# New engine lists and gate forms for a gated linear recurrence followed by a soft mixture of experts

## The chip, the cores and the metric

The kernel runs on one core of one Trainium2 chip. A core has five engines that run at the same time, each working through its own list of instructions strictly in order: TensorE (PE; its weight loads are shown apart as PEld), VectorE (DVE), ScalarE (ACT), GpSimd (POOL) and SyncE (SP), which here only issues transfers. Engines wait for each other and for transfers through semaphores. An instruction that waits holds up everything behind it in its engine's list.

The metric is the device time of one execution in microseconds (us). Less is better.

## The reference

Four sequences of 5056 tokens with 256 channels pass through a gated linear recurrence. Its output, taken as 20224 tokens, passes through a soft mixture of 8 experts with 4 slots each (32 slots).

```python
sig_r = 1.0 / (1.0 + np.exp(-r_gate))
sig_i = 1.0 / (1.0 + np.exp(-i_gate))
a_t = np.exp(8.0 * sig_r * np.log(a_base))
x_gated = np.sqrt(np.maximum(1.0 - a_t * a_t, 1e-06)) * sig_i * x
for t in range(S):
    h = a_t[:, t] * h + x_gated[:, t]
    y[:, t] = h

logits = y @ phi                               # tokens x 32 slots
d = softmax of logits over the tokens
slot_input = d.T @ y                           # 32 x 256
slot_out[e] = relu(slot_input[e] @ w1[e]) @ w2[e]   # 1024 hidden, per expert
c = softmax of logits over the slots
out = c @ slot_out
```

Everything is 32-bit floating point. The three inputs x, r_gate and i_gate have 20.7 MB each, the expert weights 16.8 MB, the output 20.7 MB.

## The kernel before

**Tiling.** The tokens are cut into 40 quads of 512 tokens (the last one is shorter). Quads are joined into 21 units: quad 0 alone, then two quads each, then the last one alone. A name such as SC7.1 means: scan, unit 7, half 1 of the 256 channels. Names with U, SR, SI, TR, TY, YC and D carry the number of a quad, names with LG, LE, LD, TE, ES, AC, AE and DM the number of one of 12 groups (nine of two units, three of one), over which the token softmax runs on.

**What is done for a quad or unit, in order.**

- Dr, Di, Dx (SP, line 708): the loads of r gate, i gate and x, 512 KB each. r and i go to seven `st` tiles, x to one of twenty double-size `b` tiles.
- TR (PE, line 781) turns the r gate so that channels lie on partitions; SR (ACT, line 792) takes its tanh; EX (ACT, line 860) makes the decay a of it.
- SI (ACT, line 807 or 805) makes the input gate from the i gate. U (line 828 or 830) multiplies it with x. TU (PE, line 902) turns the product.
- SQ (POOL or DVE, line 847) squares a; RT (ACT, line 883) takes the square root of 1 - a². ST (DVE, line 920) multiplies it with the turned product; SC (DVE, line 937) runs the recurrence as a scan along the tokens and needs the scan of the unit before it.
- TY (PE, line 960) turns the result back, YC copies it out of PSUM (ACT, line 974, or DVE, line 976).
- LG (PE, line 1022) computes the logits of a group; LE and LD, TE, ES, AC and AE carry a running maximum, exponentials and the weighted sum of tokens into the 32 slots. CT (line 1472), CM, CS, CE, RR (line 1503), RB, RC, CN, CH and CL compute the softmax over the slots and split it into two parts of lower precision.

**Behind the last scan** a serial part merges the running sums (MT to SL), runs the first expert layer (L1), relu (HS, HT, HR) and the second (L2), and makes the output table (SO to BD). The weights w10 to w27 (first digit: layer, second: expert) are loaded into `b` or `st` tiles as these come free. Then HP, HE, OT, OE (lines 1561 to 1607) compute the output and OD (line 1627) stores it.

**Four forms of the input gate.** `IV` has one letter for each quad. With D, ACT takes a tanh, and one DVE instruction with two inputs in SBUF computes (tanh + 1) times x (line 828). With P, POOL adds one first (line 818), and a plain product on POOL follows (line 830). With E, POOL multiplies tanh and x into the i gate's tile, and PE adds x while it turns the product: TU then has twice as many transposes. With S, ACT takes the sigmoid itself, from another set of its functions, and a plain product follows. The root's scale and the floor in ST go with the form.

**What sets the order.** `ORDER` (lines 91 to 160) has one written list of task names for each engine. A planner (`Planner.run`) plays these lists with a cost for each task. Its times decide which tile is given to which task, in what order the code is emitted, and where PE gets filler transposes (line 1226) while it would stand idle; the order on each engine is that of its list. Emission derives all waits from the tiles that are read and written.

```python
o = raw("i" if how == "E" else "x", q)[:, : n * D]
if how == "D":
    nc.vector.scalar_tensor_tensor(o, a, 1.0, b, op0=ALU.add, op1=ALU.mult)
else:
    eng.tensor_tensor(out=o, in0=a, in1=b, op=ALU.mult)
...
nms = ("i", "x") if gate_of(q) == "E" else ("x",)
```

## Time and profile before

| what | us |
|---|---|
| median of 3 runs | 302.67 (301.88 to 302.75) |
| the profiled execution | 304.15 |
| its span, first to last instruction | 302.4 |
| busy PE / DVE / ACT / POOL in it | 262.7 / 244.9 / 247.8 / 195.3 |

The profile is of one execution. Its span runs from the first to the last instruction, so the execution's own time is longer. Times of instructions are counted from the start of the span. Register, branch, semaphore and transfer-issuing instructions are not counted as busy. Matmuls overlap in the pipeline, so the busy time of PE is not work at peak speed. Where a row shows idle time with a releaser, the engine stood still before that instruction, and the releaser is what ended the wait.

### The profile page before, as it was taken

What the parts mean: (1) busy time and instruction counts of PE and PEld (TensorE: products, weight loads), DVE (VectorE), ACT (ScalarE), POOL (GpSimd) and SP (SyncE); (2) the same over time, 40 slices, a digit from 0 to 9 for tenths busy, and PEclk for the clock granted to TensorE, in tenths of its full rate; (3) what the DMA queues carried; (4) which work ended last, traced back from release to release, by engine and by line L of the source; (5) the groups of instructions that cost most, each with busy time, mean ns of one, the idle gap of its engine ahead of it and who ended that gap; (6) DMA issues with size and microseconds to landing.
All of it is one profiled execution on the core that took longest, in us unless ns stands there. A gap on an engine that the chain in (4) does not pass through costs nothing.

```text
span 302.4 us, 6594 instructions
## 1 busy us (share of the span) xinstructions
PE 262.7 (87%) x2635; PEld 209.1 (69%) x2635; DVE 244.9 (81%) x286; ACT 247.8 (82%) x275; POOL 195.3 (65%) x150
## 2 busy tenths in 40 slices
...
GB/s 252 411 409 391 412 400 251 359 275 337 410 408 374 315 189 210 198 353 386 400 230 337 255 299 289 413 416 386 342 422 358 2 11 406 410 415 414 417 418 260
DMA packets 23491, 100.08 MB, mean 331 GB/s; under 512 B 2850, under 2 KB 2852, under 8 KB 19364
## 3 DMA queue, kind: packets, MB, share of 16 engines
...
q14 instruction: 10, 0.08, 0.1%
...
## 4 chain that ended last, share of the span: by engine, by line
PE 33%; ACT 27%; DVE 19%; issue 8%; DMA 8%; ACTq 0%; POOL 0%; SPq 0%; DVEq 0%; POOLq 0%
DVE b L937 7%; ACT b L792 6%; ACT b L883 6%; PE pair L902 6%; PE pair L781 5%; DVE pair L920 5%; PE bank L1588 4%; ACT st L807 4%; ACT b L860 4%; DMA b<-in_moe_w_dram 3%; DMA b<-in_x_dram 3%; DMA st<-in_r_gate_dram 2%; PE one L1022 2%; PE bank L1561 2%; PE bank L1403 2%
## 5 line engine op out<-in xcount | busy, mean ns | idle before, releaser
L847 POOL TENSOR_TENSOR b<-b 128x1024 f32<-128x1024 f32 (+2 forms) x38 | 68.5, 1822 | 26.2 <-ACT b L860 26.1
L937 DVE TENSOR_TENSOR_SCAN b<-b,b,pair 128x1024 f32<-128x1024 f32 (+3 forms) x26 | 52.1, 2003 | 0.4
L781 PE MATMUL pair<-ident,st 128*128 128x128 f32 x316 | 44.1, 287 | 7.5 <-DMA st<-in_r_gate_dram 2.7
L920 DVE SCALAR_TENSOR_TENSOR pair<-b,pair 128x1024 f32<-128x1024 f32 (+2 forms) x42 | 48.4, 1155 | 2.4 <-ACT b L883 1.1
L902 PE MATMUL pair<-ident,b 128*128 128x128 f32 x316 | 44.6, 275 | 4.1 <-DVE b L828 2.7
L830 POOL TENSOR_TENSOR st<-st,b 128x1024 f32<-128x1024 f32 x17 | 40.4, 2390 | 10.2 <-DMA b<-in_x_dram 5.7
L781 PEld LDWEIGHTS pair<-ident,st 128*128 128x128 f32 x316 | 36.9, 147 | 13.7 <-DVE b L937 4.3
L960 PE MATMUL pair<-ident,b 128*128 128x128 f32 x316 | 43.9, 283 | 1.8 <-ACT b L792 0.6
L960 PEld LDWEIGHTS pair<-ident,b 128*128 128x128 f32 x316 | 38.3, 193 | 8.6 <-issue 3.0
L860 ACT ACTIVATE b<-b,ca 128x2048 f32<-128x2048 f32 (+3 forms) x28 | 44.0, 1597 | 0.0
L807 ACT ACTIVATE st<-st 128x1024 f32<-128x1024 f32 x39 | 40.5, 1067 | 3.2 <-DMA st<-in_i_gate_dram 3.2
L792 ACT ACTIVATE b<-pair 128x1024 f32<-128x1024 f32 (+1 forms) x40 | 39.9, 1018 | 3.4 <-PE pair L781 3.4
L902 PEld LDWEIGHTS pair<-ident,b 128*128 128x128 f32 x316 | 35.5, 140 | 9.5 <-issue 3.5
L937 DVE TENSOR_TENSOR_SCAN b<-b,pair 128x1024 f32<-128x1024 f32 (+5 forms) x22 | 41.5, 1892 | 0.4
L883 ACT ACTIVATE b<-b,quarter 128x2048 f32<-128x2048 f32 (+1 forms) x20 | 38.4, 1957 | 0.1
L830 POOL TENSOR_TENSOR b<-st,b 128x1024 f32<-128x1024 f32 (+1 forms) x16 | 37.0, 2314 | 0.8
L1588 PE MATMUL bank<-bd,hT 64*128 64x256 f32 x218 | 23.7, 295 | 4.3 <-DVE hT L1574 3.0
L1022 PE MATMUL one<-b,phi_sb 128*32 128x256 f32 (+1 forms) x328 | 26.5, 418 | 0.1
L1588 PEld LDWEIGHTS bank<-bd,hT 64*128 64x128 f32 x218 | 19.6, 185 | 7.4 <-ACT b L1605 2.8
L976 DVE COPY yn<-pair 128x1024 f32<-128x1024 f32 (+1 forms) x19 | 22.5, 1182 | 2.0 <-PE pair L960 1.9
L1096 PE MATMUL one<-yn,eS 128*32 128x257 f32 x296 | 21.2, 385 | 1.6 <-ACT eS L1078 1.5
L1605 ACT COPY b<-bank 128x512 f32<-128x512 f32 x28 | 15.3, 595 | 7.9 <-PE bank L1588 6.8
...
## 6 DMA issues: line engine op xcount, KB each, us to landing
...
```

The costliest lines, as they stand in the source:

```text
L781: nc.tensor.transpose(out=o[:, m, :], in_=raw("r", q)[:, m * D + h * P : m * D + (h + 1) * P], identity=ident,)
L792: nc.scalar.activation(dst, t(rp)[:, :, :c], AF.Tanh, scale=0.5)
L807: nc.scalar.activation(v, v, AF.Tanh, scale=0.5)
L830: eng.tensor_tensor(out=o, in0=a, in1=b, op=ALU.mult)
L847: eng.tensor_tensor(out=t(Nb[p])[:, h, :c], in0=v, in1=v, op=ALU.mult)
L860: nc.scalar.activation(v, v, AF.Exp, scale=ca[:, h : h + 1], bias=ca[:, h : h + 1])
L883: nc.scalar.activation(v, v, AF.Sqrt, bias=quarter if f != 1.0 else f, scale=-f)
L902: nc.tensor.matmul(o[:, m, :], raw(nm, q)[:, m * D + h * P : m * D + (h + 1) * P], ident, is_transpose=True, start=(nm == nms[0] and m == ...
L920: nc.vector.scalar_tensor_tensor(v, w, 1e-3 if gate_of(quads(p)[0]) == "S" else 0.5e-3, v, op0=ALU.max, op1=ALU.mult)
L937: nc.vector.tensor_tensor_scan(dst, dst, flat()[:, s0:s1], init, op0=ALU.mult, op1=ALU.add)
L960: nc.tensor.transpose(out=flat()[:, b * D + h * P : b * D + (h + 1) * P], in_=token(t(A[p])[:, h, : plen(p)], p)[:, :, (b0 + b) * len(quad ...
L1588: nc.tensor.matmul(t(ops[k])[:, m // 2 * D : (m // 2 + 1) * D], t(hT)[r, (b + m) * P // 2 : (b + m + 2) * P // 2], T["bd"][part][r, 0, :], ...
```

## The change

All five lists in `ORDER` are replaced, the gate forms of 16 quads change, and some of the planner's costs do. No task is added or removed; each keeps its work, apart from the gate form.

- Gate forms: 7 D, 15 P, 17 E and 1 S become 11 D, 15 P, 12 E and 2 S. New D: quads 5, 8, 12, 15 and 31; quad 9 goes from D to E. E becomes P in quads 18, 26, 28, 29 and 36, and P becomes E in 24 and 25; quad 37 goes from E to S, 38 from P to S, 39 from S to P.
- Between DVE and POOL: U5, U8, U12, U15, U31 and SQ1.0 go to DVE; U9 and SQ4.0 go to POOL.
- Between DVE and ACT: YC17, YC24 and YC30 go to ACT, YC14 and YC28 to DVE. HS0, RB7 and RB8 go to DVE, RB0, RB4 and RB10 to ACT. HE and OE of the output part are dealt out anew: DVE has 37 OE before and 34 after, ACT 43 and 46.
- Loads, among others: Di1, Di7, Di9, Dx15, Dx25 and Dr15 are issued earlier. The weights go out in another order.
- The planner's costs: SPR 1.30 to 1.29, the first load, RT and ST a little dearer, loads land 2.3 us after their end on SP instead of 2.6, and a load costs 0.13 more unless it stood ready for at least 3.2 us while SP was busy. These act on the program only through tile assignment, emission order and fillers.

The core of the diff (the lists cut to their parts that the prediction speaks of):

```diff
-IV = 'DDDDDEEDEDEPPEPPPPEEEEPPPPEEEEEPPPPEEEPS'
+IV = 'DDDDDDEDDEEPDEPDPPPEEEPPEEPEPPEDPPPEPSSP'
...
     "DVE": (
-        "CA SQ0.1 U0 SQ1.1 ST0.1 SC0.1 ST0.0 SC0.0 U2 U1 YC0.0 ST1.0 SC1.0 SQ3.0 ST1.1 U4 U3 SC1.1 ST2.0 ST2.1 SC2.0 "
-        "YC2.0 SC2.1 U7 SQ4.0 YC1.0 ST3.0 SC3.0 YC3.0 ST3.1 SC3.1 ST4.0 LE0 SC4.0 CM0 LE1 CS0 ST4.1 U9 SC4.1 CM1 CS1 "
-        "ST5.0 SC5.0 ST5.1 SC5.1 YC4.0 AE0 ST6.1 YC5.0 SC6.1 YC6.0 ST6.0 LE2 YC7.0 SC6.0 YC9.0 CM2 AE1 ST7.0 CS2 SC7.0 "
+        "CA SQ1.0 SQ0.1 U0 SQ1.1 ST0.1 ST0.0 SC0.1 U1 SC0.0 U2 YC0.0 ST1.1 SC1.1 U3 SQ3.0 ST1.0 SC1.0 U4 U7 YC2.0 ST2.0 "
+        "ST2.1 U5 SC2.1 SC2.0 ST3.1 SC3.1 YC3.0 ST3.0 U8 SC3.0 YC1.0 LE0 ST4.0 SC4.0 CM0 LE1 CS0 ST4.1 SC4.1 CM1 U12 CS1 "
+        "ST5.0 SC5.0 ST5.1 SC5.1 AE0 ST6.1 YC4.0 SC6.1 YC5.0 ST6.0 YC6.0 SC6.0 LE2 YC7.0 AE1 YC9.0 CM2 U15 ST7.0 CS2 RR1 "
+        "SC7.0 ST7.1 SC7.1 ST8.0 RR2 LE3 SC8.0 YC13.0 ST8.1 SC8.1 ST9.0 AE2 SC9.0 ST9.1 SC9.1 YC15.0 RR0 ST10.0 YC14.0 "
...
     "ACT": (
-        "SA LN SR0 EX0.1 EX0.0 SR1 SR2 SI0 EX1.0 EX1.1 RT0.0 RT1.0 SR3 SR5 SI2 SR6 SR4 SI1 EX2.0 EX2.1 SR7 SR9 SI4 SR8 "
+        "SA LN SR0 EX0.0 EX0.1 SR1 SR2 SI0 EX1.0 SI1 EX1.1 SR3 RT0.0 RT1.0 SR5 SI2 SR6 SR4 SI3 EX2.0 SR7 EX2.1 SR8 SR9 "
...
     "PE": (
-        "LG0.2 TR11 TR12 TY1.0 TU3.0 TR13 TY3.0 LG0.3 TU3.1 LG1.0 TU4.0 LG1.1 LG1.2 TR15 TR16 LG1.3 CT0 TU4.1 CT1 TR14 "
+        "TR12 LG0.0 TY3.0 TU3.0 TY1.0 LG0.1 LG0.2 LG0.3 LG1.0 TU4.0 TR15 LG1.1 LG1.2 CT0 TU4.1 LG1.3 TR16 TE1 CT1 TR14 "
...
     "SP": (
-        "Dx8 Di7 Dr12 Dr13 Di8 Dx11 Di12 Di10 Dx9 Di11 Dr16 Dx12 Dx13 Dr15 Dx10 Dr14 Dx14 Di9 Dr18 Dr17 Di14 Di13 Dr19 "
+        "Dr0 Dr1 Dr2 Di0 Di1 Dr3 Dr5 Dx0 Dx1 Dx2 Dr6 Di2 Dr4 Dr8 Di3 Dx3 Dr7 Dr9 Di7 Dx7 Di4 Di5 Di6 Dx4 Di9 Dx5 Dx6 Dr10 "
+        "Dr11 Dx8 Dr12 Dr13 Dr15 Dx15 Di8 Di12 Dx13 Di11 Dx9 Di10 Dx10 Dx25 Dr16 Dr17 Dr14 Dx11 Dx12 Dr18 Dx19 Di13 Dx20 "
...
-        "w21 Di38 Dx39 w10 Di37 Dx38 w14 w17 w24 w27 w12 w23 w13 w20 w16 w15 w26 w11 w22 w25 OD0.0 OD0.1 OD0.2 OD1.0 "
+        "Di38 Di37 w15 w17 w14 Di39 w10 w21 w25 w24 w16 w13 w11 w22 w12 w27 w20 w23 w26 OD0.2 OD0.1 OD0.0 OD1.1 OD2.1 "
...
-SPR = 1.30
+SPR = 1.29
+DRY = 0.13
+BACK = 3.2
...
+            if e == "SP":
+                if t.name[0] != "O" and now - sp_asked.pop(0, now) < BACK:
+                    dur += DRY
+                sp_asked.clear()
```

More of the change, by code (lines that the diff above doesn't have):

```diff
@@ L363, in run @@
                     if free_at[e] > now + 1e-9:
+                        if ORDER and e == "SP" and 0 not in sp_asked:
+                            t = head(e)
+                            if t is not None and t in ready[e] and can(t):
+                                sp_asked[0] = now
                         continue
@@ L713, in load @@
         own = pair and i
-        ld[(nm, q)] = add("SP", f"D{nm}{q}", SPR * n / J + (0.45, 1.15, 0.35, 0.0)[min(len(ld), 3)] + (1.2 if (nm, q) == ("x", PHI) else 0), prio=q, emit=emit, alloc=[] if own else [b], uses=[b] if own else [])
+        ld[(nm, q)] = add("SP", f"D{nm}{q}", SPR * n / J + (0.75, 1.15, 0.35, 0.0)[min(len(ld), 3)] + (1.2 if (nm, q) == ("x", PHI) else 0), prio=q, emit=emit, alloc=[] if own else [b], uses=[b] if own else [], lat=2.3)
     def raw(nm, q):
```

6 lines of the change are left out of this document (3 added, 3 removed), and 98 rows, old and new, of the table ORDER.

## The prediction

> **What bounds the kernel now.** I read the page first, then busy time by stage, then the waits and single instructions around the stages' borders. The page:
>
> ```profile
> span 302.4 us, 6594 instructions
> ...
> PE 262.7 (87%) x2635; PEld 209.1 (69%) x2635; DVE 244.9 (81%) x286; ACT 247.8 (82%) x275; POOL 195.3 (65%) x150
> ...
> GB/s 252 411 409 391 412 400 251 359 275 337 410 408 374 315 189 210 198 353 386 400 230 337 255 299 289 413 416 386 342 422 358 2 11 406 410 415 414 417 418 260
> ```
>
> The shares are means over stages with different limits. The transfer row shows three: loads up to about 234 us, two almost empty slices, and a plateau of 406 to 418 GB/s to the end. I cut the span there, and once more at 97.9 us, where DVE starts ST7.0. Columns: stretch, length, busy PE, PEld, DVE, ACT, POOL with instructions, clock, transfer share, GB/s.
>
> ```profile
> 20.00:60.00 40.00, 35.63 (x305) 28.51 (x303) 35.73 (x25) 39.90 (x35) 22.48 (x11) 1.00 0.96 365
> 60.00:97.90 37.90, 32.29 (x293) 25.85 (x294) 33.05 (x34) 33.87 (x30) 33.18 (x21) 0.95 0.96 362
> 97.90:222.50 124.60, 119.04 (x1200) 94.30 (x1199) 121.25 (x116) 122.42 (x122) 110.17 (x63) 1.00 0.86 316
> 222.50:248.50 26.00, 25.24 (x345) 16.20 (x346) 14.99 (x40) 7.58 (x20) 8.90 (x9) 1.00 0.42 176
> 248.50:302.40 53.90, 33.22 (x372) 27.61 (x369) 32.85 (x66) 27.85 (x56) 14.06 (x15) 0.86 0.94 386
> ```
>
> From 20 to 60 us ACT has 0.1 us free. From 60 to 97.9 every compute engine has 4 to 6 us free: DVE 4.85, ACT 4.03. From 97.9 to 222.5 DVE has 3.35 us free in 124.6 and ACT 2.2. From 222.5 to 248.5 a serial chain runs on PE (merge and both expert layers). From 248.5 the output stores set the end: 386 GB/s over 53.9 us, first store included. So the end moves with the time at which the last scan is done, and with little else.
>
> What leaves the second stretch idle, in order of time (the bracket gives the idle time and its releaser):
>
> ```profile
> 54.53 0.33 SPq L708 DMA_DIRECT2D st<-in_r_gate_dram  x1
> ...
> 62.08 3.59 PE L781 MATMUL pair<-ident,st 128*128 128x128 f32 x16 [2.32 <-DMA st<-in_r_gate_dram]
> ...
> 64.05 0.33 SPq L708 DMA_DIRECT2D st<-in_i_gate_dram  x1
> ...
> 66.78 0.56 DVE L1485 TENSOR_REDUCE rm<-one 128x12 f32<-128x384 f32 x1 [2.84 <-PE one L1472]
> 67.36 1.06 ACT L807 ACTIVATE st<-st 128x1024 f32<-128x1024 f32 x1 [1.29 <-DMA st<-in_i_gate_dram]
> ...
> 83.72 2.95 ACT L807 ACTIVATE st<-st 128x1024 f32<-128x1024 f32 x3 [1.86 <-DMA st<-in_i_gate_dram]
> ```
>
> The list order names them: Dr15 goes out at 54.53, TR15 waits for it on PE, CT0 stands behind TR15 and TR16, and CM0 on DVE waits 2.84 us for CT0. Di9 goes out at 64.05 and SI9 waits 1.29 us on ACT.
>
> **The change part by part.** Prices are from these groups (busy us, mean ns, then idle before):
>
> ```profile
> L828 DVE SCALAR_TENSOR_TENSOR b<-st,b 128x1024 f32<-128x1024 f32 x7 | 8.4, 1217 | 7.5 <-ACT st L807 7.5
> L830 POOL TENSOR_TENSOR st<-st,b 128x1024 f32<-128x1024 f32 x17 | 40.4, 2390 | 10.2 <-DMA b<-in_x_dram 5.7 <-ACT st L807 4.5
> L902 PE MATMUL pair<-ident,st 128*128 128x128 f32 x136 | 20.7, 275 | 1.1 <-ACT b L792 0.8 <-ACT yn L974 0.4
> L976 DVE COPY yn<-pair 128x1024 f32<-128x1024 f32 x18 | 21.8, 1210 | 2.0 <-PE pair L960 1.9
> L974 ACT COPY yn<-pair 128x1024 f32<-128x1024 f32 x21 | 20.9, 1014 | 0.0
> L1503 DVE TENSOR_REDUCE rs_all<-b 128x16 f32<-128x512 f32 x8 | 5.3, 676 | 0.5 <-ACT b L1491 0.5
> L792 ACT ACTIVATE b<-pair 128x1024 f32<-128x1024 f32 x39 | 39.3, 1028 | 3.4 <-PE pair L781 3.4
> L807 ACT ACTIVATE st<-st 128x1024 f32<-128x1024 f32 x39 | 40.5, 1067 | 3.2 <-DMA st<-in_i_gate_dram 3.2
> ```
>
> Sums of work first. POOL loses four products: 4 x 2.39 = 9.6 us. PE loses the second half of the sum of five quads: 5 x 8 transposes at 20.7/136 = 0.152 us, 6.1 us. ACT gains one y copy, 1.01 us; walking both ACT lists through the sets exp, sqrt and sigmoid gives 19 switches in each. DVE gains four products and loses one y copy: 4 x 1.217 - 1.21 = 3.7 us. Neither POOL nor PE sets the pace in the stretches above, so their 15.7 us buy nothing directly; DVE does, and it gets more.
>
> *Up to 61 us.* On ACT, SI1 and SR3 move ahead of the first root, so ST0.1 starts later by 1.07 + 1.03 = 2.1 us. In exchange U1 no longer waits: before, DVE sat idle twice for such a tanh.
>
> ```profile
> 23.09 1.23 DVE L828 SCALAR_TENSOR_TENSOR b<-st,b 128x1024 f32<-128x1024 f32 x1 [2.29 <-ACT st L807]
> 25.87 1.23 DVE L828 SCALAR_TENSOR_TENSOR b<-st,b 128x1024 f32<-128x1024 f32 x1 [1.55 <-ACT st L807]
> ```
>
> That is 3.84 us of idle time, less 2.1 us: DVE reaches ST1 1.7 us sooner. Behind it DVE takes U5 and U8 and gives SQ4.0 away (1.21 us, the row at 49.28 below), net 1.2 us; SQ1.0, now on DVE, lies in the idle start. Balance at 61 us: -0.5.
>
> *61 to 97.9 us.* DVE gets U12, U15 and the row sum RR1 and loses U9: 1.217 + 0.676 = +1.9 us. Dr15 now stands ahead of Di8 (it was nine places behind it), TR16 stands behind CT0, and Di9 stands before Dr10. If that ends the wait of 2.84 us, this stretch gives 1.9 - 2.84 = -0.9. The lower bound takes DVE's other idle time, 4.85 - 2.84 = 2.0 us, too: -2.9. The upper bound keeps the wait: +1.9. I take -0.5: nearer to the wait gone, because both loads move far, with something kept for what is late next (Di15, or an st tile that Dr15 and Di9 now hold for longer). ACT is no hindrance: RT8, RT9 and one y copy move behind RT7, which ST7.0 had to wait for.
>
> ```profile
> 90.50 3.90 ACT L883 ACTIVATE b<-b,quarter 128x2048 f32<-128x2048 f32 x2
> ...
> 95.20 2.01 ACT L883 ACTIVATE b<-b,quarter 128x2048 f32<-128x2048 f32 x1
> ...
> 97.89 1.23 DVE L920 SCALAR_TENSOR_TENSOR pair<-b,pair 128x1024 f32<-128x1024 f32 x1
> ...
> 213.74 0.63 ACT L883 ACTIVATE b<-b 128x512 f32<-128x512 f32 x1
> ...
> 217.32 0.42 DVE L920 SCALAR_TENSOR_TENSOR pair<-b,pair 128x256 f32<-128x256 f32 x1
> ```
>
> That work comes back on ACT after RT7 with the extra copy. ACT's one copy makes its last root (213.74) 1.0 us later, and ST20 at 217.32 leaves 2.9 us of room after it: no cost, and 1.0 us if that room were gone.
>
> *97.9 to 222.5 us.* From SC7.0 to the merge both DVE lists have 100 entries; they differ by U31 for one y copy (1.217 against 1.21) and by row sums and reciprocals one for one. So 121.25 us of work stay. What can move is the 3.35 us of idle time, and of that the waits for PE:
>
> ```profile
> DVE yn L976 <- PE pair L960: 0.8, 2, 0.4
> DVE pair L920 <- PE pair L902: 0.8, 3, 0.4
> ```
>
> PE loses four of its five double sums in this stretch; I let half of these 1.6 us go, -0.8. Against it stands U31, a product on DVE while POOL is busy (110 of 124.6 us). What that can cost:
>
> ```profile
> 27.89 5.73 POOL L847 TENSOR_TENSOR b<-b 128x1024 f32<-128x1024 f32 x3 [12.54 <-ACT b L860]
> ...
> 31.88 2.83 DVE L847 TENSOR_TENSOR b<-b 128x1024 f32<-128x1024 f32 x1
> ...
> 49.28 1.21 DVE L847 TENSOR_TENSOR b<-b 128x1024 f32<-128x1024 f32 x1
> ```
>
> The same square took 1.21 us at one time and 2.83 at the other, with POOL at work until 33.62. The products that DVE has now give no such case:
>
> ```profile
> L828 DVE SCALAR_TENSOR_TENSOR b<-st,b x7: 1195/1219/1227, 12.3 to 69.5; 128x1024 f32<-128x1024 f32 x7
> ```
>
> All took about 1.2 us (least, median, most in ns), five of the seven before 48 us, where POOL is half empty. So the price beside a busy POOL is bounded: 0 to 2.39 us, the whole of one POOL product. I take 0.8 for U31, half of 2.83 - 1.21. Sum of the stretch: 0.0, from -3.35 to +2.4.
>
> *From 222.5 us on.*
>
> ```profile
> 221.13 8.73 DMA b<-in_moe_w_dram
> 229.85 0.04 issue
> 229.90 2.25 PE one L1355 x33
> ```
>
> The chain of waits passes through one weight, w11, the 14th of 16 to be sent; after the change it is the 10th, and w12, wanted next, the 12th. PE waited 0.16 us there in all, so -0.2. The hidden layer's copy HS0 moves to DVE, among other work that has 11 us free in this stretch: 0, from -0.2 to +1. Behind the first store the plateau above is full: other copies and another order of stores, 0, from -0.5 to +1.
>
> **Sum:** -0.5 - 0.5 + 0.0 - 0.2 + 0 = -1.2 us on a span of 302.4. The profiled execution took 304.15 us, 1.75 more than its span, so it would be 302.95; the runs shown have a median of 302.67, 1.5 below the profiled one, so the forecast is 302.67 - 1.2 = 301.5. Its own range is 300.2 to 302.5.
>
> **The rivals.**
>
> *Products on DVE queue behind POOL (slower).* U12, U15 and U31 sit in stretches where POOL works 33.2 of 37.9 and 110.2 of 124.6 us; DVE works its list in order, so ST and SC behind a held product wait, and so does the last scan. At 1.62 us each (2.83 - 1.21) that is 4.9 us, 0.8 of it already counted: 302.67 - 1.2 + 4.1 = 305.6; at half of it 303.5. It decides if these products measure over 2 us on average. For it: the row at 31.88. Against it: POOL has 9.6 us less to do.
> The Trainium skill (SBUF — State Buffer, Who interferes with whom) says it as a rule: a DVE instruction with two SBUF inputs and a GpSimd instruction that reads SBUF share one read interface, and the second to be issued waits for the whole first. The rows at 31.88 and 49.28 agree, 2.83 against 1.21 us; that a product of this form obeys it too, no row of before shows.
>
> *The early gain is absorbed (no change).* ACT is the bound up to 60 us with 39.90 of 40 us busy, its work grows, and DVE gets 1.2 + 1.9 us more; where the idle time only moves to other waits (Di15's 1.86 us on ACT stays), the stretch up to 97.9 gives 0: 302.67 - 0.2 = 302.5.
>
> *The loads run dry (slower).* Seven st tiles hold all r and i loads, and SP waits for their release:
>
> ```profile
> SPq L708 <- PE pair L781: 56.4, 29, 5.9
> ```
>
> Di9 and Dr15, sent early and used late, take two of the seven for longer. If the load waits of ACT, 3.2 us in 60 to 97.9, double while DVE's 3.1 us stay: 302.67 + 3.2 = 305.9, decided when ACT's idle time from 20 to 98 exceeds 7 us.
>
> *It gains more.* All idle time of DVE up to 97.9 goes (-0.5 - 2.9) and half of the 3.35 after it: 302.67 - 3.4 - 1.7 - 0.2 = 297.4.
>
> **How the numbers follow.** Forecast with its neighbourhood 0.42; more gain 0.12; absorbed 0.20; products behind POOL 0.18; loads run dry 0.08. About 0.3% (0.9 us) is what a measurement of this kernel tells from no change. The forecast lies just past that bound: of its 0.42 I count 0.30 as faster and 0.12 as the same; of "products behind POOL" 0.03 is the same. More gain is faster; of absorbed, 0.05 goes to faster, 0.12 to the same and 0.03 to slower. Faster 0.47, same 0.27, slower 0.26. The range goes from 299.0, half-way to the large gain, to 304.9, past the half price of the port: about 0.1 is left out on each side.
>
> **What would show it.** Right: CM0 (first L1485 on DVE) without a wait for CT0; the first L807 wait for an i gate in 60 to 70 us gone; DVE's idle time from 20 us to SC7.0 down from about 9 to below 6 us; the stretch from SC7.0 to the merge within 2 us of 123; first store 26 us after the merge begins. Wrong: twelfth, fifteenth and thirty-first product over 2 us on DVE; ACT's load waits before 98 us above 7 us; DVE idle over 6 us after SC7.0; a first store later than 249 us.

## The result, and the profile after

| | before | changed |
|---|---|---|
| median of the compared runs, us | 302.71 (301.88 to 304.92) | 307.31 (306.88 to 307.92) |
| the profiled execution, us | 304.15 | 307.27 |
| its span, us | 302.4 | 305.4 |

The ratio is 1.0135 (95% interval 1.0086 to 1.0185). The forecast was 301.5, faster, with a range up to 304.9. The time lies outside the range and on the other side. Here and below, ratios are of the executions in the faster of the two states that a kernel shows, medians and ranges of all. In the changed file every line from the first of the functions on has a number 8 higher (L828 is L836, L920 is L928, L1485 is L1493).

The page of the changed kernel:

```profile
span 305.4 us, 6600 instructions
...
PE 266.3 (87%) x2655; PEld 212.8 (70%) x2655; DVE 243.1 (80%) x286; ACT 250.1 (82%) x279; POOL 186.1 (61%) x146
...
GB/s 254 416 409 406 362 380 287 353 337 350 406 348 381 353 203 283 222 415 282 210 251 361 335 248 399 190 413 382 425 424 302 2 83 400 407 410 405 425 269 326
```

The totals look better than before on DVE and POOL. The plateau of the stores at the end now has a hole (425, 269, 326). Busy time by stage, cut where the prediction cut it: at ST7.0 with what follows it (98.28), the merge's first transpose (224.59) and the first store (249.57). Columns as in the prediction.

```profile
20.00:60.00 40.00, 37.00 (x326) 32.26 (x324) 37.04 (x26) 38.54 (x32) 17.74 (x10) 1.00 0.97 360
60.00:98.28 38.28, 33.69 (x323) 25.91 (x321) 36.79 (x38) 37.90 (x35) 31.68 (x19) 1.00 0.97 364
98.28:224.59 126.31, 116.78 (x1164) 91.67 (x1164) 120.06 (x118) 122.61 (x124) 108.93 (x64) 0.99 0.84 314
224.59:249.57 24.98, 24.55 (x340) 15.53 (x341) 14.51 (x41) 5.94 (x17) 11.86 (x11) 1.00 0.41 169
249.57:305.40 55.83, 35.64 (x366) 29.23 (x364) 29.49 (x62) 29.27 (x59) 11.27 (x13) 0.84 0.91 372
```

DVE's idle time from 20 to 98 us went down as the prediction wanted (60.00 to 98.28: 1.5 us, before 4.85 in 37.9), and yet the scan SC7.0 begins at 99.47, before at 99.63. From there to the merge it takes 125.1 us (before 122.8), the serial part 25.0 (before 26.0), and the output 55.8 (before 53.9, at 386 GB/s, now 372). So between the two profiled executions: -0.2, +2.3, -1.0, +1.9, together the 3.0 us by which the spans differ.

The single places, from the changed kernel's DVE in order of time (start, length, instruction, in brackets the idle time ahead of it and its releaser):

```profile
30.28 1.98 DVE L836 SCALAR_TENSOR_TENSOR b<-st,b 128x1024 f32<-128x1024 f32 x1
...
42.16 2.36 DVE L928 SCALAR_TENSOR_TENSOR pair<-b,pair 128x1024 f32<-128x1024 f32 x2 [1.81 <-ACT b L891]
...
65.14 0.53 DVE L1493 TENSOR_REDUCE rm<-one 128x12 f32<-128x384 f32 x1
...
71.14 1.64 DVE L836 SCALAR_TENSOR_TENSOR b<-st,b 128x1024 f32<-128x1024 f32 x1 [0.23 <-ACT st L815]
...
96.01 1.22 DVE L836 SCALAR_TENSOR_TENSOR b<-st,b 128x1024 f32<-128x1024 f32 x1
...
99.47 2.34 DVE L945 TENSOR_TENSOR_SCAN b<-b,b,pair 128x1024 f32<-128x1024 f32 x1
103.86 1.23 DVE L928 SCALAR_TENSOR_TENSOR pair<-b,pair 128x1024 f32<-128x1024 f32 x1 [2.05 <-PE pair L910]
```

The reader sees four things. CM0 (65.14) has no wait any more. The products U3, U12 and U15 (30.28, 71.14, 96.01) cost 1.98, 1.64 and 1.22 us. ST2 has a new wait of 1.81 us at 42.16. ST7.1 has a new one of 2.05 us at 103.86, for a transpose on PE that stood behind a late load:

```profile
99.92 1.94 PE L789 MATMUL pair<-ident,st 128*128 128x128 f32 x8 [2.92 <-DMA st<-in_r_gate_dram]
```

These eight transposes took 1.94 us; in a second trace of the same kernel (below) they took 1.06, also behind a late load. Behind the idle time PE got half the clock for 3.41 us (columns as in the stage table; the third value from the right is the clock):

```profile
99.51:102.92 3.41, 3.00 (x14) 3.04 (x15) 2.30 (x2) 2.17 (x4) 3.41 (x4) 0.50 1.00 404
```

The late load is Dr22. SP issued it at 92.11. Ahead of it SP stood at Dx31, an x load that is used much later and whose tile was not yet free. Among SP's waits from 60 to 100 us (total, times, longest) it is this row's longest:

```profile
SPq L716 <- PE pair L968: 7.6, 2, 4.8
```

Dx18, Di17, Dx16, Dx23 and Dr22 stood behind it for these 4.8 us.

Between the last scan and the merge, DVE of the changed kernel, and then of the kernel before:

```profile
221.19 0.75 DVE L945 TENSOR_TENSOR_SCAN b<-b,b,pair 128x256 f32<-128x256 f32 x1
221.86 0.46 DVE L1046 TENSOR_SCALAR_CACHE_REDUCE b<-one,M 128x256 f32<-128x256 f32 x1
...
222.36 0.48 DVE L1066 TENSOR_SCALAR lD<-one,M 128x256 f32<-128x256 f32 x1
222.76 0.68 DVE L1511 TENSOR_REDUCE rs_all<-b 128x16 f32<-128x512 f32 x1
...
223.81 0.34 DVE L1046 TENSOR_SCALAR_CACHE_REDUCE b<-one,M 64x128 f32<-64x128 f32 x1
```

```profile
220.33 0.74 DVE L937 TENSOR_TENSOR_SCAN b<-b,b,pair 128x256 f32<-128x256 f32 x1
220.98 0.23 DVE L1505 RECIPROCAL rs_all<-rs_all 128x16 f32<-128x16 f32 x1
...
221.68 0.34 DVE L1038 TENSOR_SCALAR_CACHE_REDUCE b<-one,M 64x128 f32<-64x128 f32 x1
```

LE10, LD10 and the row sum RR5 now stand between the last scan and the last group's maximum LE11, where one short reciprocal stood: 2.62 us from the scan's start to LE11 instead of 1.35.

In the output part the two rows of 5 us that differ most, changed kernel first, then before:

```profile
275.00:280.00 5.00, 3.56 (x30) 3.02 (x29) 1.85 (x5) 0.76 (x2) 1.27 (x1) 0.70 0.95 395
...
290.00:295.00 5.00, 2.38 (x32) 1.91 (x30) 1.89 (x3) 3.82 (x8) 0.00 (x0) 0.91 0.46 185
```

```profile
275.00:280.00 5.00, 4.29 (x51) 3.78 (x51) 4.45 (x8) 4.00 (x8) 0.00 (x0) 1.00 1.00 416
...
290.00:295.00 5.00, 0.00 (x0) 0.00 (x0) 0.00 (x0) 0.00 (x0) 0.00 (x0) 0.50 1.01 421
```

Before, all computing was done by 290 us, and stored results stood ready. Now, from 275 to 280 us, DVE, ACT and POOL mostly stand and the granted clock is 0.70; fifteen microseconds later the stores have little to send. The chain in the changed kernel, one row of each engine:

```profile
275.13 0.52 DVE L1524 TENSOR_SCALAR st<-b 128x512 int32<-128x512 int32 x2
...
275.62 1.27 POOL L1529 TENSOR_TENSOR st<-b,st 128x512 f32<-128x512 f32 x1 [4.46 <-DVE st L1524]
...
276.95 1.09 PE L1569 MATMUL bank<-ident,st 128*128 128x128 f32 x4 [1.44 <-POOL st L1529]
```

CH7 (275.13) stands late in DVE's new list; CL7 on POOL waited 4.46 us for it, and HP7.8 on PE 1.44 us for CL7.

### The profile page after: what moved, and what is told of

The parts are those of the page before. It is cut to its first block, busy times and chain, and to the rows that moved or that the text cites. A ratio compares the mean times of both kernels' runs of the same rounds, so it can differ in the third digit from the quotient of the medians.

```text
span 305.4 us, 6600 instructions
## 1 busy us (share of the span) xinstructions
PE 266.3 (87%) x2655; PEld 212.8 (70%) x2655; DVE 243.1 (80%) x286; ACT 250.1 (82%) x279; POOL 186.1 (61%) x146
## 4 chain that ended last, share of the span: by engine, by line
PE 35%; ACT 33%; DVE 12%; issue 7%; DMA 6%; POOL 2%; SPq 1%; ACTq 0%; DVEq 0%; POOLq 0%
PE bank L1596 6%; ACT b L800 6%; DMA st<-in_r_gate_dram 6%; ACT b L891 6%; ACT st L815 5%; DVE b L945 5%; ACT b L868 5%; PE pair L910 4%; PE pair L789 4%; PE pair L968 4%; ACT yn L982 4%; PE one L1363 3%; PE bank L1411 2%; DVE pair L928 2%; ACT b L1613 2%
## 5 line engine op out<-in xcount | busy, mean ns | idle before, releaser
L855 POOL TENSOR_TENSOR b<-b 128x1024 f32<-128x1024 f32 (+2 forms) x38 | 67.9, 1804 | 34.2 <-ACT b L868 33.9
L928 DVE SCALAR_TENSOR_TENSOR pair<-b,pair 128x1024 f32<-128x1024 f32 (+2 forms) x42 | 48.2, 1155 | 8.2 <-PE pair L910 4.4
L789 PE MATMUL pair<-ident,st 128*128 128x128 f32 x316 | 43.1, 283 | 10.7 <-DMA st<-in_r_gate_dram 4.4
L910 PE MATMUL pair<-ident,b 128*128 128x128 f32 x316 | 43.3, 275 | 2.6 <-ACT yn L982 1.2
L968 PE MATMUL pair<-ident,b 128*128 128x128 f32 x316 | 43.4, 282 | 0.4 <-DVE b L945 0.2
L838 POOL TENSOR_TENSOR b<-st,b 128x1024 f32<-128x1024 f32 (+1 forms) x17 | 40.1, 2366 | 1.9 <-DMA b<-in_x_dram 1.7
L815 ACT ACTIVATE st<-st 128x1024 f32<-128x1024 f32 (+1 forms) x38 | 38.8, 1057 | 0.3 <-DMA st<-in_i_gate_dram 0.3
L891 ACT ACTIVATE b<-b,quarter 128x2048 f32<-128x2048 f32 (+2 forms) x20 | 37.0, 1891 | 0.1
L838 POOL TENSOR_TENSOR st<-st,b 128x1024 f32<-128x1024 f32 x12 | 28.7, 2391 | 9.6 <-ACT st L815 9.6
L1596 PE MATMUL bank<-bd,hT 64*128 64x256 f32 x236 | 25.1, 313 | 5.8 <-DVE hT L1582 2.7
L1613 ACT COPY b<-bank 128x512 f32<-128x512 f32 x30 | 16.9, 595 | 13.6 <-PE bank L1596 12.9
L1030 PE MATMUL one<-b,phi_sb 128*32 128x256 f32 (+1 forms) x328 | 25.9, 419 | 0.0
L1234 PE MATMUL one<-ident 128*128 128x128 f32 x138 | 24.2, 282 | 1.4 <-POOL ident masks.py:199 1.4
L982 ACT COPY yn<-pair 128x1024 f32<-128x1024 f32 x22 | 22.2, 1014 | 2.1 <-PE pair L968 2.1
```

Of the source, the lines that this page charges most:

```text
L789: nc.tensor.transpose(out=o[:, m, :], in_=raw("r", q)[:, m * D + h * P : m * D + (h + 1) * P], identity=ident,)
L815: nc.scalar.activation(v, v, AF.Tanh, scale=0.5)
L855: eng.tensor_tensor(out=t(Nb[p])[:, h, :c], in0=v, in1=v, op=ALU.mult)
L891: nc.scalar.activation(v, v, AF.Sqrt, bias=quarter if f != 1.0 else f, scale=-f)
L910: nc.tensor.matmul(o[:, m, :], raw(nm, q)[:, m * D + h * P : m * D + (h + 1) * P], ident, is_transpose=True, start=(nm == nms[0] and m == ...
L928: nc.vector.scalar_tensor_tensor(v, w, 1e-3 if gate_of(quads(p)[0]) == "S" else 0.5e-3, v, op0=ALU.max, op1=ALU.mult)
```

## The experiments

The theory after the first comparison: the loss lies in order, at three places (Dx31 ahead of Dr22; LE10, LD10 and RR5 behind the last scan; the output part), and what was gained before 100 us was taken back by new waits and more work on DVE. The rivals: DVE's added products beside POOL; the merge's order instead of its entries; chance.

**A measure first.** One execution says less than its digits. The changed kernel again, unchanged:

> The changed kernel once more, timed in five rounds beside the kernel before. Its profile and that of before differ by 3.0 us of span, the medians by 4.6 us. If the stages tell all (scan part +2.1, merge -1.0, output part +1.9), the ratio is nearer to 1.010 (305.7 on 302.7); if something outside the profiled pair adds, it stays at 1.0135 or above.

305.36 us (303.39 to 308.78, 12 runs), ratio 1.0061 (1.0025 to 1.0097). The loss is there, nearer to 2 us than to 4.6. And the kernel before again:

> The kernel before once more, unchanged: a second trace of it, and a control of how far one program differs from itself. Expected ratio 1.000 within 0.3%. In the first trace SC7.0 began at 99.63, the merge at 222.46, and from the second layer's table to the end 56.0 us passed. If these places are a property of the program, the second trace has them within 0.3 us; if the end of the recurrence scatters from execution to execution, as the kernels that share the changed recurrence did (last scan begun at 218.1 to 221.8), it lies somewhere within 1.5 us and only the last part, behind the table, stays at 56 within 0.5.

302.63 us (300.55 to 305.77), ratio 0.9984 (0.9957 to 1.0010). The second trace has its SC7.0 3.2 us earlier, at 96.43, and the rest as in the first. From the same program, DVE and PE of this second trace at the place of the wait of 2.84 us:

```profile
64.21 0.56 DVE L1485 TENSOR_REDUCE rm<-one 128x12 f32<-128x384 f32 x1 [0.59 <-PE one L1472]
...
61.16 1.94 PE L781 MATMUL pair<-ident,st 128*128 128x128 f32 x16 [1.81 <-DMA st<-in_r_gate_dram]
```

The same 16 transposes took 1.94 us here and 3.59 in the trace that the prediction read. No second load was late among them there: Dr16 had been issued ahead of Dr15, at 51.79, and the transposes followed each other without a gap. The granted clock was 0.53 over them, where the second trace has 1.00. The row of the first trace:

```profile
62.08:65.67 3.59, 3.59 (x20) 3.31 (x24) 1.86 (x1) 3.56 (x3) 3.59 (x3) 0.53 0.67 235
```

So 1.65 of the 2.84 us were a slower PE. The two kernels below that keep the recurrence of before (e2_new_tail, e6_merge) have 0.23 and 1.07 us at CM0. So the 2.84 us that the forecast took away belonged to that execution, not to the kernel; about 0.6 was to be had.

Steps of the profiles by group (means, us; first scan = begin of SC0; the end is the table BD00 to the last instruction):

| group (profiles) | first scan | CM0 | SC7.0 | SC7.0 to last scan | last scan to first layer |
|---|---|---|---|---|---|
| recurrence of before (before, before_again, e2_new_tail, e6_merge) | 17.5 | 64.9 | 97.6 | 121.5 | 8.3 (e2, e6: 10.4, 10.4) |
| changed (after, after_again, e1, e4, e5, e10) | 20.5 | 65.2 | 99.7 | 120.9 | 8.9 to 9.1 |
| changed, Dx31 later (e3, e7, e7 again, e13, e14, e15) | 20.1 | 65.0 | 99.5 | 119.2 | 8.9 to 9.1 |

**The output part.** Old order of all engines from the table (SO, HE0.0, CL1, first OD) on, else the changed kernel:

```diff
-"DVE": "... SO HE0.8 SH BD10 OE0.8 RB8 CH4 ... CH7 CH11 OE6.8 ..."
+"DVE": "... SO RC6 SH BD10 CH6 OE0.0 OE0.4 ..."   # and ACT, PE, POOL, SP likewise
```

> The changed kernel up to the scaling of the expert output, and from there on the old order of all five engines. Theory: the new output order starves the stores near the end (185 GB/s from 290 to 295 us), so the old order gives back 1.9 us: first store to end 54 us instead of 55.8, ratio to the changed kernel 0.994. Rival: the stores fill a fixed plateau and the late gap is an accident of PE's clock in that execution; then the ratio to the changed kernel is 1.000.

305.19 us, ratio 1.0055 (1.0028 to 1.0081); from BD00 to the end 55.8 us in its profile, against 57.9 and 57.8 in those of the changed kernel. The place is confirmed by the stage; the total moved by less than its interval. The two late instructions alone:

```diff
-"DVE": "... OE5.10 CH7 CH11 OE6.8 ..."
+"DVE": "... HE8.8 CH7 CH11 OE5.12 OE8.8 HE6.8 OE5.10 OE6.8 ..."
```

> The changed kernel with two short DVE instructions moved: CH7 and CH11 right behind HE8.8, some 4 us earlier. Theory: they hold back CL7 on POOL, HP7.8 on PE (1.44 us of wait at 276 us) and so the granted clock (0.70 from 275 to 280 us); with them early PE stays at 1.00, and first store to end falls from 55.8 to 54 to 54.5 us, ratio to the changed kernel 0.995. Rival: the gap comes from the order of the stores and the copies around it; then less than 0.5 us changes and the clock still falls.

305.57 us, 1.0059 (1.0029 to 1.0089), 56.4 us to the end, and POOL's wait for CH7 0.40 instead of 4.46. That wait is cured. But other kernels with the changed output order (e5, e3, e2, e10, e8) came out at 56.7, 57.1, 56.2, 56.8 and 57.6, and the wait for CH7 is there in all five (4.2 to 4.8 us), also in the one with 56.2. All kernels with the old order, twelve profiles, lie at 55.5 to 56.3. So the new order as a whole costs about 1.3 us (57.1 without e4_ch7 against 55.8 on the mean). How much of it is CH7 stays open, but the clock goes with the order. In all eight profiles with the changed output order it is 0.50 for 3.4 or 6.8 us at a time, once or twice, while outputs are still computed; in e4_ch7 too, from 281.88 to 285.29 us. In the twelve with the old order it falls once, in the last 2 us of PE's work or behind it.

**The other way round:** the kernel before up to the last scan, with the changed order from the merge on.

```diff
-"DVE": "... LD11 AE9 MX MR YC39.0 WJ W ..."      # old, from LD11, RT20.0, MT, U39, w25 on
+"DVE": "... LD11 RC0 RR5 AE9 MX MR WJ YC39.0 W ..."  # else the order of the changed kernel
```

> The kernel before up to the last running maximum, and from there on the new order of all engines (merge, expert layers and output). Theory: the new merge order is 1.0 us shorter and the new output order 1.9 us longer, so 303.4 + 0.9 = 304.3; from the merge's first transpose to the output table 23.0 us instead of 23.9, from the table to the end 57.9 instead of 56.0. Rival: what follows the merge is set by how the recurrence left the tiles and the clock, then this kernel is equal to before, 303.4, with 56.0 us behind the table.

306.61 us, 1.0103 (1.0067 to 1.0139): as large a loss as the whole change, with the recurrence untouched. Its first layer begins 10.4 us behind the last scan instead of 8.3. The merge only, with the old output part behind it:

```diff
-"DVE": "... LD11 AE9 MX MR YC39.0 WJ W ..."
+"DVE": "... LD11 RC0 RR5 AE9 MX MR WJ YC39.0 W ... RR6 RR8 SO RC6 SH BD10 CH6 ..."   # changed merge, old order from SO on
```

> The kernel before with only the new order of the merge and the expert layers; recurrence and output as before. Theory: 1.0 us faster than before, 302.4 (ratio 0.997), and so faster than both kernels. Rival: the gain in the merge is taken back by later weights or a later first store; then 303.4, ratio 1.000.

304.78 us, 1.0063 (1.0030 to 1.0096), again 10.4. The traces show where the 2.1 us lie. RC0 and RR5, which the changed list has ahead of LE11, had to go behind LD11 here, ahead of the merge's own entries AE9, MX and MR: the merge's first matrix product (MC) begins 2.59 us behind its first transpose, before 1.75. From there to the first layer it takes 5.7 us instead of 4.4, and for 3.4 us of that PE has half the clock, in e2_new_tail as here and in e6_merge from 224.72 to 228.14:

```profile
225.45:228.86 3.41, 3.41 (x23) 1.07 (x22) 1.72 (x5) 0.81 (x4) 0.46 (x1) 0.50 1.02 430
```

In both traces of the kernel before and in both of the changed kernel the clock is 1.00 there. So these two runs show the price of this mixture of lists, and not that of the changed merge in its own kernel. Counted from the last scan, the table BD00 comes 25.9 and 26.1 us later in the kernel before and 26.3 in the changed one; the 1.0 us that the serial part seemed to gain was waiting done earlier, ahead of the merge.

**RR5.** (RR5 is the row sum of the fence above.)

```diff
-"DVE": "LE10 LD10 RR5 LE11 LD11 AE9 ... AE10 AE11 RR7"   -"ACT": "YC37.0 RB5 DM11 ES10"
+"DVE": "LE10 LD10 LE11 LD11 AE9 ... AE10 AE11 RR5 RR7"   +"ACT": "YC37.0 DM11 ES10 ... DM10 RB5"
```

> The changed kernel with one reciprocal (RR5) moved behind AE11 on DVE and its copy RB5 behind DM10 on ACT, nothing else. If the three entries between the last scan and the last group's maximum cost 1.2 us because RR5 waits there and holds them up, the time from the last scan's begin to the merge falls from 3.4 to below 2.8 us, the total by 0.5 to 1.2 us against the changed kernel (ratio to before near 1.003). If the merge waits for ACT's exponentials anyway, the merge begins earlier but the first layer does not, and the total stays at 1.006.

306.93 us, 1.0108 (1.0079 to 1.0138). The merge begins 2.8 us behind the last scan instead of 3.4, and the first layer 9.0 behind it, where the changed kernel has 8.9: the rival was right, the 0.6 us is lost again at once. So this row was read rightly and its price was nothing.

**The load.**

```diff
-"SP": "... Dr21 Dx31 Dx18 Di17 ... Di26 Dx32 ..."
+"SP": "... Dr21 Dx18 Di17 ... Di26 Dx31 Dx32 ..."
```

> The changed kernel with one load moved: Dx31 goes to its place ahead of Dx32, so that SP no longer stands 4.8 us for a free tile with Di17, Dx16 and Dr22 behind it. Theory: TR22 finds its load, the waits of 2.9 us on PE and 2.05 us on DVE near 100 us go, and the merge begins 1 to 2 us earlier (223 instead of 224.6), ratio to the changed kernel 0.995. Rival: DVE has the same work and another load is late next; the merge begins within 0.5 us of 224.6, ratio 1.000.

304.45 us, 1.0065 (1.0029 to 1.0102). Its DVE has no wait at ST7.1. From SC7.0 to SC7.1 it takes 3.49 us here; in the six profiles with Dx31 in its new place it takes 3.50 to 5.70 (4.8 on the mean), in all eight with Dx31 later and the changed gates 3.49 to 3.50. Of the six, the three with half the clock there (the first trace of the changed kernel, e4_ch7, e10_root) took 5.5 to 5.7, the others 3.5 to 4.5: part of the price is the late load, part the clock behind it. The mechanism is shown, and the group's stretch to the last scan is 1.7 us shorter. One kernel's total doesn't tell 1.7 us from nothing.

**All three mends:** Dx31 later, RR5 and RB5 later, the output in the order of before.

```diff
-"SP": "... Dr21 Dx31 Dx18 ..."   -"DVE": "LE10 LD10 RR5 LE11 ..."   -"DVE": "... SO HE0.8 SH ..."
+"SP": "... Di26 Dx31 Dx32 ..."   +"DVE": "... AE11 RR5 RR7 ..."     +"DVE": "... SO RC6 SH BD10 CH6 ..."
```

> The changed kernel with all three suspected places mended: Dx31 sent later, the row sum RR5 (and the bias RB5 on ACT) moved from ahead of the last running maximum to behind the merge, and the old output order. Theory: 0.5 to 1 us from the load, 0.7 us from RR5, 1.1 us from the output, 305.7 - 2.5 = 303.2, level with before. Rival: DVE's extra 3.7 us of work set the recurrence's length; then only the output's 1.1 us comes back, 304.6.

302.98 us, 0.9999 (0.9966 to 1.0032). And again:

> The changed kernel with all three mends (Dx31 later among the loads, RR5 and RB5 later, the output part in the order of before) once more. If the loss lies in these places, the ratio to before is again between 0.996 and 1.003, and below that of the next kernels' common base, the changed kernel (1.006 to 1.013). If the first result was chance, it comes out at 1.006.

302.93 us, 1.0012 (0.9984 to 1.0040). The loss is gone, twice; with RR5 worth nothing, the load and the output order carry it. Nothing is left of the planned gain either.

**Is it the work moved to DVE?** Gates 12, 15 and 31 back to POOL, all else as changed:

```diff
-IV = 'DDDDDDEDDEEPDEPDPPPEEEPPEEPEPPEDPPPEPSSP'
+IV = 'DDDDDDEDDEEPPEPPPPPEEEPPEEPEPPEPPPPEPSSP'
-"DVE": "... U12 ... U15 ... U31 ..."
+"POOL": "... P112 LD0 U12 LD1 ... P115 LD2 U15 ... P131 ... U31 ..."
```

> The changed kernel with the gate forms of quads 12, 15 and 31 back from D to P: three sums and three products go from DVE to POOL, at about their old places; all else as in the changed kernel. Theory of too much work on DVE: DVE's 3.65 us less shorten the recurrence by 2 to 3.6 us, 305.7 - 2.8 = 302.9. Rival (late loads and waits for PE set the pace, DVE would only wait longer): within 0.7 us of the changed kernel, 305.7; if POOL's 10.6 us more hold the products back, slower, up to 307.

315.56 us, 1.0407 (1.0365 to 1.0449). This tells of where I put an instruction, not of DVE's work. P112 stood ahead of LD0 and waited for the tanh SI12, and everything behind it waited too. POOL, then DVE:

```profile
70.97 1.12 POOL L826 TENSOR_SCALAR st<-st,one_sb 128x1024 f32<-128x1024 f32 x1 [7.28 <-ACT st L815]
72.06 0.58 POOL L1062 TENSOR_SCALAR lD<-b,M 128x384 f32<-128x384 f32 x1
...
72.68 0.56 DVE L1496 TENSOR_TENSOR b<-one,rm 128x384 f32<-128x384 f32 x1 [6.60 <-POOL lD L1062]
```

Put better, on the mended kernel, with quad 9's product on DVE again as before:

```diff
-"DVE": "... ST4.1 SC4.1 CM1 U12 CS1 ... CM2 U15 ST7.0 ..."    # IV: 9 E, 12 D, 15 D
+"DVE": "... ST4.1 U9 SC4.1 CM1 CS1 ... CM2 ST7.0 ..."         # IV: 9 D, 12 P, 15 P
+"POOL": "... P111 U11 P112 U12 SQ8.0 ... U13 P115 U15 LD2 ..."
```

> The mended kernel with the gate forms of quads 9, 12 and 15 as before: product 9 (1.2 us) on DVE again, products 12 and 15 and their additions (2.4 and 1.1 us each) on POOL again, behind the product they followed there. DVE has 1.2 us less up to 100 us, POOL 4.6 us more in a stretch where 33 of 39.5 us are busy. Theory that DVE's own list sets the pace there: SC7.0 begins 0.5 to 1.2 us earlier and the total falls by up to 1 us against the mended kernel. Rival, that POOL then becomes late and DVE waits for its products: SC7.0 begins later than 99.5, and the total is 303 to 306.

305.93 us, 1.0084 (1.0064 to 1.0105). The rival was right: DVE has less to do and waits for POOL's products and what stands behind them; SC7.0 at 101.12.

```profile
99.92 0.69 DVE L1496 TENSOR_TENSOR b<-one,rm 128x512 f32<-128x512 f32 x1 [1.34 <-POOL lD L1062]
```

But the two traces of the mended kernel show that the products on DVE can cost. Their SC7.0 begins at 102.01 and 98.32 us. DVE's U15 and the POOL product beside it, e7_mended first, then e7_again:

```profile
96.54 3.22 DVE L836 SCALAR_TENSOR_TENSOR b<-st,b 128x1024 f32<-128x1024 f32 x1
...
96.32 2.36 POOL L838 TENSOR_TENSOR b<-st,b 128x1024 f32<-128x1024 f32 x1
```

```profile
94.86 1.22 DVE L836 SCALAR_TENSOR_TENSOR b<-st,b 128x1024 f32<-128x1024 f32 x1
...
94.97 3.34 POOL L838 TENSOR_TENSOR b<-st,b 128x1024 f32<-128x1024 f32 x1
```

Where POOL's product began 0.22 us earlier, U15 took 2.0 us longer; where U15 began 0.11 us earlier, POOL's product took 1.0 us longer. U15 took 3.22 to 3.25 us in three of the fourteen profiles that have it on DVE (e7_mended, e11_merge, e12_all), and 1.21 to 1.50 in the others.

**The merge restored, and the wait at 42 us.** First the order of before from the last scan on, with LE10 and LD10 ahead of it:

```diff
-"DVE": "... ST20.0 SC20.0 LE10 LD10 RR5 LE11 ..."
+"DVE": "... ST20.0 LE10 LD10 SC20.0 RC1 LE11 ..."   # then all engines as before; Dx31 later
```

> The changed kernel with Dx31 later among the loads, the last group but one (LE10, LD10) ahead of the last scan as before, and the order of before on all engines from the last scan to the end. If the order there cost 0.6 us, the first layer begins 8.3 us behind the last scan's begin, not 8.9 to 9.1, and the ratio is 0.994 to 1.000, below the mended kernel's 1.000 and 1.001. If ACT's backlog from the changed recurrence costs it, 8.9 or more stay and the ratio is again 1.000.

305.73 us, 1.0061 (1.0023 to 1.0098). The first layer comes 8.5 us behind the last scan (8.3 expected), and the kernel is slower than the mended one: LE10 waits for its logits, and the last scan behind it.

```profile
222.65 0.48 DVE L1046 TENSOR_SCALAR_CACHE_REDUCE b<-one,M 128x256 f32<-128x256 f32 x1 [1.28 <-PE one L1030]
```

(SC7.0 also came late in this execution, at 102.72, with U15 at 3.25 us.) Then the wait of ST2, on the changed kernel alone and, with the same edit, on the one above:

```diff
-"ACT": "... SI7 RT3.0 RT2.0 SI5 ..."    -"POOL": "... SQ2.0 SQ3.1 SQ2.1 U6 ..."
+"ACT": "... SI7 RT2.0 RT3.0 SI5 ..."    +"POOL": "... SQ2.0 SQ2.1 SQ3.1 U6 ..."
```

> The changed kernel with the root RT2.0 ahead of RT3.0 on ACT and its square SQ2.1 ahead of SQ3.1 on POOL, nothing else. If the wait of ST2.0 (1.2 to 1.8 us at 42 us) is what ate the gain of the earlier tanh, the wait is gone, CM0 begins at 63.4 to 64.2 instead of 65.1, SC7.0 at 98 to 99 and the ratio to before falls from 1.006 to 1.013 to about 1.003. If DVE's added work sets the pace, the time only moves to the next wait: CM0 at 64.5 to 65.1, SC7.0 at 99 to 100.5, ratio 1.006 or more.

> The kernel of e11_merge with the root and square of e10_root ahead as well. If each named place is a cause of its own, the sum is 1.8 (loads) + 1.2 (output) + 0.6 (merge) + 1 to 1.8 (root) against the changed kernel, and this is 1 to 2 us faster than before: ratio 0.993 to 0.998. If the places take each other's gain, it stays within 0.3% of before.

306.54 us, 1.0104 (1.0051 to 1.0158), and 304.81 us, 1.0059 (1.0026 to 1.0092). The wait stayed, though the root that ST2.0 needs was done 2 us earlier. DVE, ACT and PE of e10_root:

```profile
42.39 2.36 DVE L928 SCALAR_TENSOR_TENSOR pair<-b,pair 128x1024 f32<-128x1024 f32 x2 [1.27 <-ACT b L891]
...
38.45 3.91 ACT L891 ACTIVATE b<-b,quarter 128x2048 f32<-128x2048 f32 x2
...
40.38 1.91 PE L910 MATMUL pair<-ident,b 128*128 128x128 f32 x16
```

The releaser that the row names is the one that ended last by the profile: the second root ends at 42.36, but PE's transposes TU2.1 and TU2.0, behind a row of fillers, end at 42.29 as well. Two things ended together; taking one away gave nothing. So TU2.0 first, on the mended kernel with that root and its square ahead, and then without the fillers ahead of it:

```diff
-"PE": "... TY2.0 TU2.1 TU2.0 TR10 ..."
+"PE": "... TY2.0 TU2.0 TU2.1 TR10 ..."
```

> The mended kernel (Dx31, RR5, output part) with the root RT2.0 and square SQ2.1 ahead and, on PE, TU2.0 ahead of TU2.1. If ST2.0 waits for the transposes of its own half, they end 0.95 us earlier and the wait at 42 us falls from 1.2 to 1.8 us to 0.3 to 0.9; CM0 begins 43.7 us behind the begin of the first scan, where every kernel with the changed recurrence so far had 44.67 to 44.70. If it waits for something else, 44.7 stays. At the end at most 0.9 us, so the ratio is 0.996 to 1.003.

```diff
-elif e == "PE" and self.warm_from <= now < self.warm_to:
+elif e == "PE" and self.warm_from <= now < self.warm_to and (t is None or t.name != "TU2.0"):
```

> The same with no filler transposes on PE between TY2.0 and TU2.0 (about ten pairs of them left out there). If the fillers hold TU2.0 up, TU2.0 runs at 38 to 39.5 us, the wait is gone, CM0 begins 42.9 to 43.4 us behind the first scan, and if the 1.3 to 1.8 us reach the end the ratio is 0.993 to 0.999. If another wait takes its place, 43.7 stays as in the kernel above.

303.27 us, 1.0029 (0.9994 to 1.0064), and 304.10 us, 1.0043 (1.0009 to 1.0076). DVE of the first, then of the second:

```profile
41.04 2.36 DVE L928 SCALAR_TENSOR_TENSOR pair<-b,pair 128x1024 f32<-128x1024 f32 x2 [0.56 <-PE pair L910]
44.26 1.23 DVE L836 SCALAR_TENSOR_TENSOR b<-st,b 128x1024 f32<-128x1024 f32 x1 [0.86 <-ACT st L815]
```

```profile
40.26 2.34 DVE L928 SCALAR_TENSOR_TENSOR pair<-b,pair 128x1024 f32<-128x1024 f32 x2
44.48 1.23 DVE L836 SCALAR_TENSOR_TENSOR b<-st,b 128x1024 f32<-128x1024 f32 x1 [1.88 <-ACT st L815]
```

The wait at ST2 shrinks to 0.56 and to nothing, and DVE stands as much longer one instruction on, at U5, which the change put on DVE and whose tanh SI5 stands on ACT behind the roots. From the first scan to CM0 it takes 44.90 and 44.91 us; in the changed kernel 44.69. The last step, U5 behind SC2.1:

```diff
-"DVE": "... ST2.0 ST2.1 U5 SC2.1 SC2.0 ST3.1 ..."
+"DVE": "... ST2.0 ST2.1 SC2.1 U5 SC2.0 ST3.1 ..."
```

> The kernel of e14_nofill with U5 behind SC2.1 on DVE instead of ahead of it. If the product's place holds DVE up, SC2.1 begins at 42.6 instead of 45.6 us, U5 has no wait above 0.2 us, ST3.1 begins 1.5 us earlier, CM0 43.0 to 43.6 us behind the first scan instead of 44.9, and SC7.0 and the end come 0.5 to 1.8 us earlier than in that kernel: ratio 0.995 to 1.002. If a further wait takes its place, 44.5 or more stay between first scan and CM0.

302.83 us, 0.9991 (0.9956 to 1.0026). U5 has no wait, SC2.1 begins at 42.16, and ST3.1 waits (DVE, then PE):

```profile
50.53 1.23 DVE L928 SCALAR_TENSOR_TENSOR pair<-b,pair 128x1024 f32<-128x1024 f32 x1 [2.65 <-PE pair L910]
...
45.70 1.09 PE L789 MATMUL pair<-ident,st 128*128 128x128 f32 x8 [2.25 <-ACT b L800]
```

45.79 us from the first scan to CM0, where 43.0 to 43.6 were expected. Of the 2.65 us some 1.3 are the clock: it was 0.50 from 46.88 to 50.30 us, and the three rows of four transposes that ST3.1 waits for took 1.06 us each, where e14_nofill has 0.60 to 0.66. So two waits were taken away and each time the next took its whole place; what the third step is worth at full clock, this trace doesn't tell. At the end of the row PE's transposes wait for ACT, which in the changed kernel is busy 38.54 of 40 us there. No version was found that is measurably faster than before.

## Why the prediction was wrong, step by step

Two terms failed. For the time up to SC7.0 the prediction summed -1.0 us, by taking 2.84 us of a wait off as if the kernel had it in every execution; the groups of profiles show +2.1. The output part was put at 0, and they show +1.3.

**Up to 61 us, -0.5 forecast.** The tanh that came earlier did what was said: at the scan SC1.1 the changed kernel is 1.6 us ahead (28.01 against 29.62 for the same content; 1.7 forecast), although ST0.1 came 2.5 us later on the mean of the groups and not 2.1, and the first scan 3.0, as it now stands behind ST0.0 too. But behind 28 us the new wait of 1.81 us and U5 and U8 took it back. At CM0, the wait there left out, the changed kernels are 1.5 us later (65.2 against 63.7 on the mean). The step failed by what it left out: ST2 and U5 wait for ACT, which was shown as full in the first row of the prediction. Its new list has RT2.0 behind RT3.0, and U5, whose tanh stands behind both roots there, was put ahead of a scan. That is the rival "the early gain is absorbed", in this stretch; it gave no change, and the truth was worse.

**61 to 97.9 us, -0.5 forecast.** "If that ends the wait of 2.84 us": it ended (65.14, no wait), and the wait of the SI9 row went too. Between the two profiled executions the stretch from 60 us on did gain. But the wait was of one execution (0.23 to 1.07 in three others), while the added work of 1.9 us is in all of them. From CM0 to SC7.0 it takes 32.7 us on the mean of the kernels of before and 34.5 of the changed ones: +1.8, close to the work alone. This is the term that turned the sign. DVE's whole balance from the first scan to SC7.0, in the same means: 74.6 us of work against 72.8, +1.8; the first scan 3.0 us later; idle time 4.7 against 7.4 us, 2.7 less. Together that is the +2.1 at SC7.0. The prediction read the 2.84 us as the wait for a load; 1.65 of them were PE's clock, whose mean of 0.95 stands in its own row of that stretch. It had written that its profiled execution lay 1.5 us above the median, and had not asked which of the waits were that 1.5 us.

**97.9 to 222.5 us, 0.0 forecast.** 120.9 against 121.5 us to the last scan (120.8 in the two traces of the kernel before alone): right in size, inside -3.35 to +2.4. Inside it stand 1.3 to 1.7 us lost behind Dx31, and without that loss the stretch would have gained 2.3 (1.6 against those two traces), more than the 0.8 that fewer transposes were given. The Dx31 loss is the mechanism of "the loads run dry", though not where that rival put it: the st tiles and ACT's waits were not it (ACT's load waits came to 0.3 us), but an x load ahead of its tile's release on SP, with a wanted r load behind it. "Row sums and reciprocals one for one" was wrong behind the last scan: 1.3 us later at the merge, 0.6 at the first layer. e5_rr5 and e11_merge say that neither moving RR5 nor restoring the order gets this back.

**Products on DVE beside POOL, +0.8 counted and a rival.** In the profiled execution it fell. All eleven products of the changed kernel, least, median and most in ns:

```profile
L836 DVE SCALAR_TENSOR_TENSOR b<-st,b x11: 1201/1220/1984, 15.5 to 182.1; 128x1024 f32<-128x1024 f32 x11
```

U31, given 0.8, took 1.22 us, and U12 and U15 1.64 and 1.22: under the 2 us from which the rival was to decide. U3 (1.98, the first row of the long fence above) ran into this POOL square:

```profile
29.28 1.89 POOL L855 TENSOR_TENSOR b<-b 128x1024 f32<-128x1024 f32 x1 [17.59 <-ACT b L868]
```

It ended at 32.26, 1.09 after POOL's end. By the rule of the Trainium skill (SBUF — State Buffer, Who interferes with whom) that the second of two such instructions waits for the whole first, it would have ended some 1.2 us after it; the trace agrees. The mechanism is therefore right, and most products meant no loss because POOL stood idle or began later. Where U15 did begin second it cost 2.0 us, more than the 1.62 that the rival gave; that is a part of the spread from execution to execution, and not of the loss between the two profiled ones.

**From 222.5 us on, -0.2 and 0 forecast.** "Other copies and another order of stores, 0, from -0.5 to +1": about +1.3 by the groups, +1.9 between the two profiled executions; the largest single error outside the early part. The plateau was read as full, which made the computing behind it look free. It was full because all computing was done at 288 us, 14 us before the end (in the changed kernel at 294, 11 before it), and an order that spends this lead, in waits like CH7's, lets the stores run dry.

**The list of what would show it.** CM0 and the i gate wait: right. DVE's idle time from 20 us to SC7.0: 4.5 us, below 6, right. It gained next to nothing: between the two profiled executions DVE idles 4.7 us less from the first scan to SC7.0, but the first scan begins 2.7 us later and 1.8 us more work follows. SC7.0 to the merge within 2 us of 123: wrong, 125.1. First store 26 us after the merge: 25.0. Among the signs of being wrong: DVE idle after SC7.0 6.0 us in 100 to 220 (before 3.0), at the bound named; first store 249.6, later than 249. These two came true; the products and ACT's load waits did not. In the working, half-way from 301.5 to the large gain's 297.4 is 299.4 and not 299.0; nothing hangs on it.

By the groups of profiles: +2.1 up to SC7.0, -0.6 to the last scan, +0.6 to the first layer, -0.3 through both layers, +1.3 in the output, +3.1 together; the two spans of the changed kernel are 305.4 and 303.7, those of before 302.4 and 299.3. Why SC7.0 comes 2 to 3 us later in some executions of one program, the traces show in the main. Of the 3.2 us between the two of the kernel before (99.63 and 96.43), 2.25 are the wait at CM0, most of it PE's clock. Of the 3.7 between the two of the mended kernel (102.01 and 98.32), 2.0 are U15 behind POOL and 1.0 an earlier first scan.

The clock also goes with the times of the changed kernel. Its sixteen runs took 303.4 to 304.7 us where the clock granted over the run was 0.978 to 0.980 (four runs), 305.1 to 305.8 at 0.968 to 0.971 (four), and 306.9 to 308.8 at 0.969 or less (eight, all four of the first comparison among them). So the 2 us between its two comparisons go with the clock. What decides in one execution whether a pause of PE costs the clock, and which of DVE and POOL begins first, stays open: no run here sets either.
